# One TensorE run per chunk: x rows, state products, scores, log sums and transposes on small tiles, from the 11th chunk on

## The chip, the cores and the metric

The kernel runs on one core of one Trainium2 chip. The metric is the device time of one execution in microseconds (us). The time before the change is 608.76 us, the median of three runs between 608.49 and 609.51.

## What is computed

The first part is a gated linear recurrence over 768 steps for 4 batches of 8 heads of width 48; the second part is a layer with 2048 hidden units over all 3072 rows.

```python
f = 1.0 / (1.0 + np.exp(-f_logit))
for t in range(S):                       # q, k, v, f_logit: (4, 8, 768, 48)
    state = f[:, :, t, :, None] * state + np.einsum('bhd,bhe->bhde', k[:, :, t], v[:, :, t])
    y[:, :, t] = np.einsum('bhd,bhde->bhe', q[:, :, t], state)
x = y.transpose(0, 2, 1, 3).reshape(B * S, H * D)     # (3072, 384)
h = x @ w_in                                          # w_in (384, 2048)
sp = np.maximum(h, 0.0) + np.log1p(np.exp(-np.abs(h)))
out = (h * erf(sp)) @ w_out                           # w_out (2048, 384)
```

All of it is fp32.

## The kernel before

The rows are cut into 24 chunks of 128 steps (six per batch), and two chunks make a block of 256 rows, so there are 12 blocks. For each chunk the recurrence is worked out in matrix form, in two halves of 64 steps. These are the stages of one chunk `g`, with the lines under which the profile shows them:

- **Log sums** (`log_sums`, L396): one 128x128 by 128x384 matmul with the triangular matrix `tri` sums the logarithms of the gates `lt` over each half. `decays` (L400, L401) are two exponentials of it on ScalarE, and VectorE multiplies them into q (`times_q`, L414) and k (`times_k`, L421). `send_totals` (L408) sends the totals of the halves out with eight small DMAs on SP's queue.
- **Transposes** (`transposes`, L437): eight 128x128 transposes turn the decayed q and k into columns. ScalarE copies q (`copy_q`, L443), VectorE copies k (`copy_k`, L451).
- **State products** (`state_products`, L499): k times v, sixteen 64x48 matmuls on tiles of 64 rows and 64 columns of TensorE; the results lie in the PSUM tile `sc`, one bank for each half. **Scores** (`scores`, L510): sixteen 48x64 matmuls into the same tile. VectorE masks the scores (L537) and adds up the state (`add_state`, L475 and L476), and GpSimd copies the state into `sv` (`copy_state`, L481). The state of the second half is put off in `late` and runs ahead of a later stage.
- **Rows of x** (`x_rows`, L580): 32 matmuls of 128 rows by 32 columns give the chunk's output, called `y`; `copy_x` (L591) copies it on ScalarE into `xT`.

The second part works on blocks. `hidden` (L671) gives the 2048 hidden units of a block in four groups of 12 matmuls; ScalarE copies each group out of PSUM (L683), and `act_steps` takes it through the activation on ScalarE and VectorE in small steps. `project` (L822) makes the output of a block with 56 products of 128x192. Hidden groups and outputs use one pool of two PSUM buffers of two banks, `ps_moe`; log sums, transposes and y use another, `ps_at`, of two buffers of one bank.

The order is written out by hand (`manual_schedule`), so every engine gets its instructions in the order of the source. The first chunks follow a list of tokens (`EARLY`). After it, an iteration `it` runs the output products of block `it - 2` and the hidden groups of block `it + 1`, and after each matmul, a slot `s`, the loop may put in something else: a step of an activation, a sum for the output stage, a load, or a stage of the chunks of block `it + 2`. From block `ADJACENT = 5` (chunk 10) on, the stages stand at these slots of the 104 of an iteration, where `stage_y_s` is the x rows of a chunk, followed directly by state products and scores of the next one:

```python
todo += [(stage_y, g)] if last else [(stage_d, g + 1), (stage_t, g + 1), (stage_y_s, g)]
at = [0, 1, 15, 24, 31, 52, 66] if it + 2 == ADJACENT else [2, 26, 42, 54, 76, 90]
```

The last chunk's y stands at slot 54 of the ninth iteration, among the last output products. Loads of q, k, v and of the gate logits (`load`, `load_f`) and of v into `sv` (`load_sv`, L256) go through SP's queue in the order in which they are issued.

Of the kernel before, what the change touches and what calls it, by code (L numbers as in the profile page):

```python
# [70 lines left out]
P = 128  # L71
# [3 lines left out]
def kernel(  # L75
# [44 lines left out]
    for i, a in enumerate(a for _, a, _ in SERF_KAB):  # L120
        nc.vector.memset(serf_bias[:, i : i + 1], a)

    def heads(src, b, c):
        return src[b, :, c * P : (c + 1) * P, :].rearrange("h t d -> t h d")

# [49 lines left out]
    epool = main.enter_context(tc.tile_pool(name="epool", bufs=2))  # L175
    work1 = main.enter_context(tc.tile_pool(name="work1", bufs=1))
    ps_sc = main.enter_context(tc.tile_pool(name="ps_sc", bufs=1, space=PSUM))
    ps_at = main.enter_context(tc.tile_pool(name="ps_at", bufs=2, space=PSUM))
    ps_moe = main.enter_context(tc.tile_pool(name="ps_moe", bufs=2, space=PSUM))

    sc_all = ps_sc.tile([P, 2, 512], FP32, name="sc", tag="sc")

# [35 lines left out]

    FIRST, TOTALS = 3, 6


    lts = {}

    def load_f(g):
        b, c = divmod(g, NCH)
        blk, j = divmod(g, CPB)
        if blk not in lts:
            lts[blk] = lpool.tile([P, CPB, d_model], FP32, name="lt", tag="lt")
        nc.sync.dma_start(
            out=lts[blk][:, j, :].rearrange("t (h d) -> t h d", d=D), in_=heads(f_logit, b, c)  # L230
        )

    def load(g, what="qkv", queue=None):
        b, c = divmod(g, NCH)
# [4 lines left out]
        if "v" in what:  # L239
            queue.dma_start(  # L240
                out=vts[g % NV][:].rearrange("t (h d) -> t h d", d=D), in_=heads(v, b, c)
            )

    def half(c):
        return slice(C * c, C * (c + 1))

    def copy_sv(g, r, c):
        pairs = vts[g % NV][half(c)].rearrange("t (a r d) -> t a r d", r=2, d=D)
# [141 lines left out]
    def log_sums(g):  # L390
        blk, j = divmod(g, CPB)
        if g < FIRST:
            dTs[g] = pair_tile()[:, 0, 0:d_model]
        else:
            dTs[g] = ps_at.tile([P, 512], FP32, name="ps_d", tag="at")[:, 0:d_model]
        nc.tensor.matmul(dTs[g], lhsT=tri[:], rhs=lts[blk][:, j, :], start=True, stop=True)  # L396

    def decays(g):
        ps = dTs.pop(g).rearrange("t (h d) -> t h d", d=D)
        nc.scalar.activation(out=dps[g % 2][:, :, 0:D], in_=ps, func=AF.Exp, scale=-1.0)  # L400
        nc.scalar.activation(out=kds[g % 2][:, :, 0:D], in_=ps, func=AF.Exp)  # L401

    def send_totals(g):
        dp = dps[g % 2]
# [17 lines left out]
            out=kd, in0=kns[g % NQ][:].rearrange("t (h d) -> t h d", d=D), in1=kd, op=ALU.mult  # L422
        )

    def stage_d(g):
        log_sums(g)
        decays(g)
        send_totals(g)
        times_q(g)
        times_k(g)  # L430

    def transposes(g, n):
        src = qd if n == "q" else kds[g % 2]
        tps[g, n] = ps_at.tile([P, HP, P], FP32, name="ps_t", tag="at")
        flat = src[:].rearrange("t (a r) d -> t a (r d)", r=2)
        for a in range(HP):
            nc.tensor.transpose(tps[g, n][:, a, :], flat[:, a, :], ident[:])  # L437

    def copy_q(g):
        qAs[g] = work.tile([P, 2, HP, P], FP32, name="qA", tag="qA")  # L440
        ps = tps.pop((g, "q"))
        for r in range(2):
            nc.scalar.copy(out=qAs[g][half(r), r], in_=ps[half(r)])  # L443

    def copy_k(g):
        kTs[g] = work1.tile([P, HP, P], FP32, name="kT", tag="kT")
        ps = tps.pop((g, "k"))
        if g < 9:
            nc.scalar.copy(out=kTs[g][:], in_=ps[:])
        else:  # L450
            nc.vector.tensor_copy(out=kTs[g][:], in_=ps[:])  # L451

    def stage_t(g):
        if g - 1 in late:
            late.pop(g - 1)()
        transposes(g, "q")
        transposes(g, "k")
        copy_q(g)
        copy_k(g)

# [28 lines left out]
    def no_state(g):  # L489
        for r in range(2):  # L490
            nc.gpsimd.memset(svs[g % NSV][rows(r), r, 0, :, PAD : PAD + D], 0.0)
# [57 lines left out]
    def stage_s(g):  # L549
        n = g % NCH  # L550
        if n == 0:
            no_state(g)
        state_products(g)
        scores(g)
        for c in range(2):
            for r in range(2):
                mask(g, c, r)
                if c == 1 and by_select(g):
                    select(g, r)
        next_state(2 * g)  # L560
        if n < NCH - 1:
            late[g] = lambda: next_state(2 * g + 1)

    def x_rows(g, c):
        if c == 0:
            yts[g] = (
                pair_tile()[:, 0, 0 : n_k * P].rearrange("t (k n) -> t k n", k=n_k) if g < 2
                else ps_at.tile([P, n_k, P], FP32, name="y", tag="at")
            )
        y, qA, sv = yts[g], qAs[g], svs[g % NSV]  # L570
        todo = {i: [] for i in range(P // M)}
        for kt in range(n_k):
            for i in todo:
                a, part = divmod(kt * (P // M) + i, 3)
                for r, o in {0: ((0, PAD),), 1: ((0, PAD + M), (1, 0)), 2: ((1, M),)}[part]:
                    todo[i].append((kt, a, r, o))
        for n in range(len(todo[0])):
            for i in todo:
                kt, a, r, o = todo[i][n]
                nc.tensor.matmul(  # L580
                    y[M * i : M * (i + 1), kt, half(c)], lhsT=sv[:, r, c, a, o : o + M],
                    rhs=qA[:, r, a, half(c)], start=(c == 0 and n == 0), stop=True,
                    skip_group_check=True,
                )
# [8 lines left out]
    def stage_y(g):  # L593

        if g in late:
            late.pop(g)()
        x_rows(g, 0)
        x_rows(g, 1)
        copy_x(g)

    def stage_y_s(g):

        stage_y(g)
        stage_s(g + 1)


    acts = deque()
# [180 lines left out]
    def project(blk):  # L788
# [7 lines left out]
        }.items()}  # L796
        first = [1, 2, 5, 3]
        if end:
            place[4] = ps_at.tile([P, 512], FP32, name="ops4", tag="at")[:, 0:DH]
            first.append(4)  # L800

        def pair(n):
# [79 lines left out]
    def check_decays():  # L882

        low = work.tile([P, 1], FP32, name="low", tag="low")
        nc.vector.tensor_reduce(
            out=low[:], in_=Tall[:].rearrange("p g c a -> p (g c a)"), axis=AX.X, op=ALU.min
        )
        yield
        ps = ps_at.tile([P, 512], FP32, name="ps_f", tag="at")
        nc.tensor.transpose(ps[0:1, 0:P], low[:], ident[:])  # L890
        low1 = work.tile([1, 1], FP32, name="low1", tag="low1")
        nc.vector.tensor_reduce(out=low1[:], in_=ps[0:1, 0:P], axis=AX.X, op=ALU.min)
        nc.vector.tensor_scalar(
            out=flag[0:1, :], in0=low1[:], scalar1=GUARD, scalar2=None, op0=ALU.is_lt
        )
        yield
# [84 lines left out]
    with tc.manual_schedule():  # L981
# [39 lines left out]
            if to_load and home_free(to_load[0]):  # L1021
                load_piece(to_load.pop(0))

        def load_to(g):
            while loaded[0] <= min(g, n_chunks - 1):
                load(loaded[0])
                loaded[0] += 1


        LOOK = 3  # L1030
        loaded = [2 * ADJACENT + 1]

        nc.vector.memset(sc_all[:, :, HP * C : HP * (C + D)], 0.0)
        busy.append(ps_moe.tile([P, 2, 512], FP32, name="busy", tag="moe")[:, 0, 0:P])
        early()

        def stages(blk):
            todo = [(stage_s, blk * CPB)] if blk == ADJACENT else []
            for g in range(blk * CPB, (blk + 1) * CPB):
                last = g == n_chunks - 1  # L1040
                if blk >= ADJACENT:
                    todo += [(stage_y, g)] if last else [(stage_d, g + 1), (stage_t, g + 1), (stage_y_s, g)]
                    continue
                todo += [] if last else [(stage_d, g + 1)]
                todo += [(stage_s, g)]
                todo += [] if last else [(stage_t, g + 1)]
                todo += [(stage_y, g)]
            return todo

        check = check_decays()  # L1050
        due = 0.0
        for it in range(2, n_blocks):
            gen, n = slots(it)
            todo = stages(it + 2) if it + 2 < n_blocks else []
            at = [int(3 + (n - 13) / max(1, len(todo)) * i) for i in range(len(todo))]
            if ADJACENT <= it + 2 < n_blocks:

                at = [0, 1, 15, 24, 31, 52, 66] if it + 2 == ADJACENT else [2, 26, 42, 54, 76, 90]
                at = at[: len(todo)]
            if it + 3 < n_blocks:  # L1060
                prepare_at = at[todo.index((stage_d, (it + 3) * CPB))] - 14
            at, todo = deque(at), deque(todo)
            for s, _ in enumerate(gen):
                due += 0.6
# [5 lines left out]
                if at and s == at[0]:  # L1070
                    at.popleft()
                    f, g = todo.popleft()
                    f(g)
                    if f in (stage_y, stage_y_s):
                        if g + NSV < n_chunks:
                            load_sv(g + NSV)
                        load_to(g + LOOK)
                if s == n // 2 and it + 4 < n_blocks:
                    for j in range(CPB):
                        load_f((it + 4) * CPB + j)  # L1080
                if it + 3 < n_blocks and s == prepare_at - 6:
                    clamp(it + 3, 0, CPB)
                if it + 3 < n_blocks and s == prepare_at:
                    logs(it + 3, 0, CPB)
                if it < 4:
                    step = s % 7 in (1, 4)
                elif it == n_blocks - 1:
# [236 lines left out]
```

## Time and profile before

The execution under the profiler took 610.34 us; its span on the core is 608.6 us, so some 1.7 us lie around it.

| engine | busy us | share of the span |
|---|---|---|
| TensorE (PE) | 590.3 | 97% |
| weight loads (PEld, beside PE) | 517.1 | 85% |
| VectorE (DVE) | 430.2 | 71% |
| ScalarE (ACT) | 382.8 | 63% |
| GpSimd (POOL) | 92.3 | 15% |

| group of TensorE | records | busy us |
|---|---|---|
| hidden units (L671) | 1152 | 259.7 |
| x rows y (L580) | 1408 | 25.4 |
| log sums (L396) | 48 | 19.6 |
| scores (L510) | 768 | 16.3 |
| state products (L499) | 704 | 14.0 |
| transposes of k, of q (L437) | 96, 96 | 15.1, 14.6 |

A record is one instruction on the engine: an fp32 matmul makes two, a transpose one. Busy times of records overlap where several tiles of the array work at once, so a group's busy time is not what it takes away from the rest; for that, the starts in the timeline are compared. Idle time of an engine counts only where TensorE waits for it.

### The profile page before, as it was taken

How to read it: one execution, taken by the hardware profiler on the slowest of the kernel's cores; microseconds unless marked ns; L12 is line 12 of the kernel's file. 1: busy time of each engine (PE TensorE's matmuls, PEld its weight loads, DVE VectorE, ACT ScalarE, POOL GpSimd, SP SyncE). 2: the span in 40 equal slices, each digit the busy share in tenths (PEclk: the TensorE clock that was granted, in tenths of full speed). 3: DMA queues.
4: the chain of work that ended last, by engine and by line, in shares of the span. 5: the costliest groups of instructions: out<-in, count | busy, mean ns of one | idle time of the engine just before them, and what ended most of it. 6: DMA issues, size and time to landing. Idle time of an engine off the chain costs nothing.

```text
span 608.6 us, 13919 instructions
## 1 busy us (share of the span) xinstructions
PE 590.3 (97%) x5769; PEld 517.1 (85%) x5769; DVE 430.2 (71%) x705; ACT 382.8 (63%) x483; POOL 92.3 (15%) x119
## 2 busy tenths in 40 slices
PE   8999999998899999999999999999999899999995
PEld 7788888886566789889989889989989789989995
DVE  4789889976975876867776677767686575648451
ACT  6738859787836687757757766857676446366000
POOL 1330342120404010220021200112011200000000
PEclk9999999999899999999999999999999999999998
DMA  9799966206130430520421421412310000000000
GB/s 187 211 234 238 236 146 128 32 2 156 32 74 2 99 59 1 105 53 3 89 57 14 79 57 24 80 41 40 54 41 1 2 26 1 27 1 2 27 26 30
DMA packets 152148, 41.34 MB, mean 68 GB/s; under 512 B 143888, under 2 KB 146960, under 8 KB 152080
## 3 DMA queue, kind: packets, MB, share of 16 engines
q1 hardware_dynamic: 149856, 39.81, 29.9%
q8 instruction: 47, 0.77, 0.5%
q10 hardware_dynamic: 2224, 0.59, 0.4%
q14 instruction: 21, 0.17, 0.1%
HBM read 35.59 MB, written 4.72 MB: 66 GB/s over the span
## 4 chain that ended last, share of the span: by engine, by line
PE 82%; DVE 6%; ACT 6%; DMA 2%; issue 1%; POOL 1%; SPq 1%; ACTq 0%; DVEq 0%; POOLq 0%
PE hps L671 36%; PE ops L822 25%; PE ops L771 6%; PE y L580 3%; PE ps_t L437 3%; PE ps_d L396 2%; PE sc L510 2%; PE sc L499 2%; PE busy L380 1%; ACT x L160 1%; DMA w_out_sb<-in_moe_w_out_dram 1%; DVE e L165 1%; POOL sv L481 1%; DVE qA L537 1%; DVE Hg L628 1%
## 5 line engine op out<-in xcount | busy, mean ns | idle before, releaser
L671 PE MATMUL hps<-xT,w_in_sb 128*128 128x256 f32 x1152 | 259.7, 383 | 2.4 <-ACT Hg L683 1.7
L671 PEld LDWEIGHTS hps<-xT,w_in_sb 128*128 128x128 f32 x1152 | 217.6, 191 | 34.5 <-ACT Hg L683 2.1
L165 DVE SCALAR_TENSOR_TENSOR e<-x,e 128x1024 f32<-128x1024 f32 x96 | 117.4, 1223 | 15.7 <-ACT x L160 15.3
L481 POOL COPY sv<-state 48x192 f32<-48x192 f32 x88 | 75.8, 861 | 340.7 <-DVE state L476 245.6
L160 ACT ACTIVATE x<-Hg,serf_bias 128x1024 f32<-128x1024 f32 x88 | 97.5, 1141 | 0.2
L157 ACT ACTIVATE e<-Hg 128x1024 f32<-128x1024 f32 x44 | 46.5, 1058 | 57.3 <-DVE Hg L628 57.1
L822 PE MATMUL ops<-wT,Hg 128*128 128x192 f32 x320 | 78.5, 329 | 0.0
L683 ACT COPY Hg<-hps 128x1024 f32<-128x1024 f32 x44 | 44.4, 1010 | 42.7 <-PE hps L671 42.5
L628 DVE TENSOR_TENSOR Hg<-Hg,e 128x1024 f32<-128x1024 f32 x44 | 53.7, 1221 | 24.5 <-ACT e L625 24.4
L822 PE MATMUL ops<-wT,scratch 128*128 128x192 f32 x288 | 67.9, 327 | 0.9 <-DVE scratch L830 0.9
L822 PE MATMUL ops<-w_out_sb,Hg 128*128 128x192 f32 x320 | 65.1, 326 | 0.0
L822 PEld LDWEIGHTS ops<-wT,Hg 128*128 128x128 f32 x320 | 55.8, 190 | 1.9
L822 PEld LDWEIGHTS ops<-w_out_sb,Hg 128*128 128x128 f32 x320 | 54.6, 190 | 2.0
L537 DVE TENSOR_TENSOR qA<-sc,tri 64x256 f32<-64x256 f32 x68 | 28.7, 422 | 35.7 <-PE sc L510 31.6
L625 ACT ACTIVATE e<-e 128x1024 f32<-128x1024 f32 x48 | 50.4, 1051 | 2.9 <-DVE e L165 2.8
L822 PEld LDWEIGHTS ops<-wT,scratch 128*128 128x128 f32 x288 | 50.3, 190 | 1.1 <-issue 1.1
L830 DVE TENSOR_TENSOR scratch<-scratch,ops 128x384 f32<-128x384 f32 (+1 forms) x40 | 19.9, 497 | 34.1 <-ACT scratch L838 26.6
L443 ACT COPY qA<-ps_t 64x512 f32<-64x512 f32 x48 | 27.8, 578 | 13.1 <-PE ps_t L437 12.7
L414 DVE TENSOR_TENSOR qd<-qn,dp 128x384 f32<-128x384 f32 x24 | 13.9, 579 | 28.6 <-ACT dp L400 28.6
L822 PE MATMUL ops<-w_out_sb,scratch 128*128 128x192 f32 x132 | 32.3, 326 | 0.0
L580 PEld LDWEIGHTS y<-qA,sv 128*32 128x32 f32 x1408 | 21.2, 110 | 8.7 <-issue 5.4
L838 ACT COPY scratch<-ops 128x192 f32<-128x192 f32 x10 | 3.2, 318 | 39.2 <-PE ops L822 39.2
(123 smaller groups left out, 692.6 us busy)
## 6 DMA issues: line engine op xcount, KB each, us to landing
lt<-in_f_logit_dram SPq DMA_DIRECT2D x24, 192.0 KB, 3.8
qn<-in_q_dram SPq DMA_DIRECT2D x24, 192.0 KB, 3.9
kn<-in_k_dram SPq DMA_DIRECT2D x23, 192.0 KB, 3.5
vt<-in_v_dram SPq DMA_DIRECT2D x23, 192.0 KB, 4.0
out_dram<-scratch SPq DMA_DIRECT2D x11, 384.0 KB, 2.6
sv<-in_v_dram SPq DMA_DIRECT2D x84, 48.0 KB, 2.9
w_out_sb<-in_moe_w_in_dram SPq DMA_DIRECT2D x4, 768.0 KB, 7.3
Hg<-in_moe_w_in_dram SPq DMA_DIRECT2D x4, 768.0 KB, 6.4
```

Of the source, the lines that this page charges most:

```text
L157: nc.scalar.activation(out=dst[:], in_=h, func=AF.Exp)
L160: nc.scalar.activation(out=dst[:], in_=h, func=AF.Tanh, bias=serf_bias[:, i : i + 1], scale=SERF_KAB[i][0])
L165: nc.vector.scalar_tensor_tensor(out=e[:], in0=x[:], scalar=SERF_KAB[i][2], in1=e[:], op0=ALU.add, op1=ALU.mult)
L481: nc.gpsimd.tensor_copy(out=svs[g1 % NSV][rows(r), r, c1, :, PAD : PAD + D], in_=state[rows(r)])
L537: nc.vector.tensor_tensor(out=to, in0=sc[half(c), r], in1=tri1[half(c)].unsqueeze(1).broadcast_to((C, HP, C)), op=ALU.mult,)
L580: nc.tensor.matmul(y[M * i : M * (i + 1), kt, half(c)], lhsT=sv[:, r, c, a, o : o + M], rhs=qA[:, r, a, half(c)], start=(c == 0 and n == 0 ...
L625: nc.scalar.activation(out=e[0][:], in_=e[0][:], func=AF.Tanh, scale=SERF_C)
L628: nc.vector.tensor_tensor(out=h, in0=h, in1=e[0][:], op=ALU.mult)
L671: nc.tensor.matmul(hts[blk, gi][:, j, :], lhsT=w_in_sb[:, kt, ft * P : (ft + 1) * P], rhs=xTs[blk][:, kt, :], start=(kt == 0), stop=(kt == ...
L683: nc.scalar.copy(out=gr["h"], in_=hts.pop((blk, gi))[:])
L771: nc.tensor.matmul(ops[:, tt, 0:d_model], lhsT=gr["h"][:, j, tt * P : (tt + 1) * P], rhs=w_out_sb[:, ft, :], start=(ft == 0), stop=(ft == ...
L822: nc.tensor.matmul(place[n], lhsT=x[:, j, :], rhs=y, start=(gi == 0 and j == 0 and n in first), stop=(gi == n_g - 1 and j == 1), skip_grou ...
```

## The change

From chunk 10 on, one function `burst(g)` replaces the three places of a chunk. It issues on TensorE, one after the other, the x rows of chunk `g`, the state products and scores of `g + 1`, the log sums of `g + 3` and the transposes of `g + 2`. It stands at two slots of an iteration: after the first hidden group of 12 matmuls and after the last slot.

- The log sums of chunks 13 to 23 are four matmuls of 64x64 tiles with 192 columns each, into a buffer of `ps_moe`. For this the gate logits lie otherwise in `lt`: four heads in each half of the partitions, the two halves of the chunk beside each other, loaded with four DMAs in place of one. Chunks 11 and 12 keep the former log sums.
- The transposes of chunks 11 to 23 are sixteen of 64 rows, into two banks, one for each half. Those of chunk 11 stand alone at slot 15 of the third iteration, as before.
- The two one-bank buffers `ps_at` are closed before chunk 11 and one buffer of two banks, `ps_at2`, takes their place; y lies in its first bank, the transposes in both.
- The loads of q and k run one chunk further ahead, those of the gate logits about an iteration, and the state of the second half is updated eight slots after the run.

Everything up to the state products of chunk 10 keeps its order. The core of the diff:

```diff
+    singles = ExitStack()
+    ps_at = [singles.enter_context(tc.tile_pool(name="ps_at", bufs=2, space=PSUM))]
+    def bank(name):
+        if len(ps_at) == 1:
+            return ps_at[0].tile([P, 512], FP32, name=name, tag="at")
+        return bank_pair(name)[:, 0, :]
+    def bank_pair(name):
+        return ps_at[1].tile([P, 2, 512], FP32, name=name, tag="at2")
+    def open_pair():
+        singles.close()
+        ps_at.append(main.enter_context(tc.tile_pool(name="ps_at2", bufs=1, space=PSUM)))
...
+    MERGE = 2 * ADJACENT
+    SPLIT = MERGE + 3
...
+        if g < SPLIT:
+            nc.sync.dma_start(out=lt.rearrange("t (h d) -> t h d", d=D), in_=heads(f_logit, b, c))
+            return
+        w = d_model // 2
+        for n in range(2):
+            for u in range(2):
+                t0 = c * P + u * C
+                nc.sync.dma_start(
+                    out=lt[half(n), w * u : w * (u + 1)].rearrange("t (h d) -> t h d", d=D),
+                    in_=f_logit[b, HP * n : HP * (n + 1), t0 : t0 + C, :].rearrange("h t d -> t h d"),
+                )
...
+    def tiled_sums(g):
+        blk, j = divmod(g, CPB)
+        w = d_model // 2
+        dTs[g] = ps_moe.tile([P, 2, 512], FP32, name="ps_d", tag="moe")[:, :, 0:w]
+        for i in range(2):
+            for c in range(2):
+                n = (c + i) % 2
+                nc.tensor.matmul(
+                    dTs[g][half(c), n, :], lhsT=tri1[half(n), :],
+                    rhs=lts[blk][half(n), j, w * c : w * (c + 1)], start=True, stop=True,
+                )
...
+    def tiled_transposes(g):
+        ps = bank_pair("ps_t")
+        for i, src in enumerate((qd, kds[g % 2])):
+            part = ps[:, :, HP * C * i : HP * C * (i + 1)]
+            for a in range(HP):
+                for c in range(2):
+                    nc.tensor.transpose(
+                        part[:, c, C * a : C * (a + 1)], pairs(src)[half(c), a, :],
+                        ident[half(c), half(c)],
+                    )
+            tps[g, "qk"[i]] = part.rearrange("p c (a t) -> p a c t", a=HP)
...
-    def stage_y_s(g):
-        stage_y(g)
-        stage_s(g + 1)
+    def burst(g):
+        if g in late:
+            late.pop(g)()
+        x_rows(g, 0)
+        x_rows(g, 1)
+        s, t, d = (n < n_chunks for n in (g + 1, g + 2, g + 3))
+        if s:
+            if (g + 1) % NCH == 0:
+                no_state(g + 1)
+            state_products(g + 1)
+            scores(g + 1)
+        if d:
+            tiled_sums(g + 3)
+        copy_x(g)
+        if t:
+            tiled_transposes(g + 2)
+        if s:
+            masks(g + 1)
+        if d:
+            decays(g + 3)
+            send_totals(g + 3)
+        if t:
+            copy_q(g + 2)
+            copy_k(g + 2)
+        if d:
+            times_q(g + 3)
+            times_k(g + 3)
...
+            first = [(stage_s, g), (stage_d, g + 1), (stage_t, g + 1), (stage_d, g + 2)]
+            return (first if blk == ADJACENT else []) + [(burst, g), (burst, g + 1)]
...
+            loads, logits_at = {n - 20: it + 5}, {36: it + 4}
+            if it == 3:
+                loads[6], logits_at = it + 4, {8: it + 3, 34: it + 4}
...
-                at = [0, 1, 15, 24, 31, 52, 66] if it + 2 == ADJACENT else [2, 26, 42, 54, 76, 90]
+            if it >= 3:
+                if it == 3:
+                    open_pair()
+                at = ([0, 1, 15, 24] if it == 3 else []) + [n - 1 - 3 * n_h // 4, n - 1]
...
+                        load_to(g + LOOK)
+                        load_to(g + LOOK + (f is burst), 1)
+                        late_at = 8
...
+                if it >= 3 and late and not late_at:
+                    late.pop(min(late))()
+                late_at -= 1
```

## The prediction

> **What bounds the kernel now.** I read the busy shares first, then the slices, then the waits of TensorE, then TensorE's timeline around one chunk. The page says who is full:
>
> ```profile
> PE 590.3 (97%) x5769; PEld 517.1 (85%) x5769; DVE 430.2 (71%) x705; ACT 382.8 (63%) x483; POOL 92.3 (15%) x119
> ...
> PE   8999999998899999999999999999999899999995
> ```
>
> TensorE is busy in nearly every slice, and the chain that ended last is 82% PE. From 210 us on, which is all of the stretch that the change touches, its own waits are two:
>
> ```profile
> PE y L580 <- POOL sv L481: 1.6, 1, 1.6
> PE ops L822 <- DVE scratch L830: 0.9, 1, 0.9
> ```
>
> So time moves only by TensorE work that gets shorter or longer, by the first of these waits, or by a new wait. The timeline shows what one chunk costs TensorE (start, length, engine, line, tiles, shape, records; an fp32 matmul is two records, a transpose one):
>
> ```profile
> 305.02 0.60 PE L437 MATMUL ps_t<-ident,qd 128*128 128x128 f32 x4
> 305.46 0.60 PE L437 MATMUL ps_t<-ident,kd 128*128 128x128 f32 x4
> 305.90 6.21 PE L671 MATMUL hps<-xT,w_in_sb 128*128 128x256 f32 x28
> 312.04 1.10 PE L580 MATMUL y<-qA,sv 128*32 128x64 f32 x64
> 313.07 0.57 PE L499 MATMUL sc<-vt,kd 64*48 64x48 f32 x32
> 313.46 0.66 PE L510 MATMUL sc<-qA,kT 48*64 48x64 f32 x32
> 314.05 5.88 PE L671 MATMUL hps<-xT,w_in_sb 128*128 128x256 f32 x26
> ...
> 320.74 0.81 PE L396 MATMUL ps_d<-lt,tri 128*128 128x384 f32 x2
> 321.39 0.81 PE L822 MATMUL ops<-w_out_sb,Hg 128*128 128x192 f32 x4
> ```
>
> Differences of starts are the true cost, since lengths overlap. The eight transposes: 305.90 - 305.02 = **0.88 us**. The log sums: 321.39 - 320.74 = **0.65**. The run of y, state products and scores: 314.05 - 312.04 = 2.01, plus its edges. A hidden record takes 0.216 us (25 records in 299.63 to 305.02 on the same timeline), so 28 end at 311.94 and y starts 0.10 late; the 26 records after it take 5.72 in place of 5.61, another 0.11. Together **2.2**. One chunk: 2.2 + 0.88 + 0.65 = 3.73 us.
>
> How parallel are small tiles here? A hidden record streams 256 columns in 0.216 us, 0.84 ns a column, so 64 columns are 54 ns. The 64 y records take 1.03 us less a change of tile shape of about 0.1: 14.5 ns each, 3.7 at a time. The state products: 0.39 / 32 = 12.2 ns against 48 columns at 40 ns, 3.3 at a time. Four 64x64 tiles do run side by side.
>
> **What the Trainium skill says.** "TensorEngine Tiling (Array Packing)", Key Properties: changing the tiling mode drains TensorE, and different tiles may load weights and multiply in parallel. The trace agrees with both: about 0.1 us before y, 0.1 from y to the state products, 0.1 after the return, none between state products (64*48) and scores (48*64), and the 3.3 to 3.7 at a time above. The same page, Gotcha 1 of Restrictions and Gotchas: row tiles must write different PSUM banks. State products do so now (the two halves of `sc`), and the new forms do too (banks n and c). "TensorE: Matmul & The Clock Gate", LDWEIGHTS: a weight load takes about columns / 1.2 ns, whatever the rows. The groups agree (110, 121, 135, 190 ns for 32, 48, 64, 128 columns: 0.83 ns a column over a fixed 83), but the transposes' own loads are 142 ns for 128 columns: 59 over the fixed part, so these stream twice as fast. The same page, Part 1: a gate halves the clock after a window of little work, about 3.4 us. Here once late:
>
> ```profile
> 482.00:486.00 4.00, 2.75 (x38) 2.23 (x39) 2.03 (x4) 2.61 (x4) 1.44 (x2) 0.82 0.01 4
> 486.00:490.00 4.00, 4.00 (x16) 3.32 (x15) 3.93 (x7) 1.75 (x2) 0.00 (x0) 0.75 0.28 100
> ```
>
> The column after POOL is the granted clock. It falls right after y of chunk 23 waited 1.61 us at 483.15 for the state copy on POOL, and costs 4 x 0.18 + 4 x 0.25 = 1.7 us.
>
> **The change part by part.** (a) Log sums of chunks 13 to 23 (11): one 128x384 matmul becomes four of 64x64 with 192 columns. Two records of 192 x 0.84 = 162 ns per tile, four tiles at once: 0.33 us, a gain of 0.32 each. If only two run at once it is 0.65, no gain. No row shows four 64x64 tiles with 192 columns; the state products and scores are nearest, and I take their parallelism.
>
> (b) Transposes of chunks 11 to 23 (13): eight of 128 rows become sixteen of 64 rows and 64 moving columns, on two row tiles. Streaming alone is 8 x 54 ns = 0.43; loads of 59 ns per tile with some 6 ns between (scores: (0.59 - 0.11) / 8 = 60 ns a group of four for 54) give 8 x 65 = 0.52. If loads of the two row tiles don't overlap it is 16 x 59 = 0.94, slightly worse than now. I take 0.52: gain 0.36 each.
>
> (c) Edges. The run keeps those of today and adds one, from 64x64 to 64-row tiles with 128 columns, ahead of the transposes: unseen, between 0 (the state products and scores switch freely) and 0.2 (the dearest edge's two parts); I take the 0.13 of the known ones. Chunk 11's transposes stand alone between 128x128 work and pay both outer edges, 0.3.
>
> (d) Sum: 11 full runs (chunks 10 to 20) x (0.32 + 0.36 - 0.13) = 6.05; the run of chunk 21 has no log sums: 0.36 - 0.13 = 0.23; chunk 11's transposes 0.36 - 0.3 = 0.06. Together **6.3 us** off TensorE, all on the path. The bounds are 13 x 0.45 + 11 x 0.32 - 0.3 = 9.1, with the new edge free, and -13 x 0.06 - 12 x 0.2 - 0.3 = -3.5.
>
> (e) Placement. Runs now stand after the first hidden group and after the last one. Chunk 23's y comes 36 hidden matmuls (36 x 0.43 = 15.6 us) after chunk 22's, not 12 products (3.9 us). The state copies let y go on at 483.15, 8.4 us after chunk 22's y began at 474.79, so the wait goes: **1.6 us**. With it probably the half clock: 1.7 in this execution. But the execution shown took 610.34 (span 608.6 and 1.7 around it), 1.6 above the median of 608.76, and the unprofiled runs may lack that window, so I count half: **0.85**.
>
> (f) New waits in a run. Transposes need both banks that y held, so they wait for ScalarE's copy of y. Ahead of that copy stands the copy of the hidden group (1.01 us), which starts about 0.2 after the group's last record streams, and y's own copy (0.48) may then start at 1.2 us into the run and ends at 1.75. TensorE gets to the transposes at 0.1 + 1.03 + 0.39 + 0.48 + 0.33 + edges = 2.4. Cover 0.65 us; ScalarE was idle before most group copies (42.5 us over 26). Gone, it costs the excess, up to one activation of 1.15 us. The log sums take a hidden/output PSUM buffer: its last readers are VectorE's final sums of the output stage, over 7 us earlier. The next hidden group needs the buffer of the first, free after 1.2 us, inside the run. The reverse wait, for the two decay activations, has 5.2 us of hidden matmuls over it.
>
> (g) Other engines. Copies, decays, masks and sums keep their sizes. VectorE gets them in a lump (masks 4 x 0.42, state 0.75, key copy 0.69, products 1.13: 4.3 us) that puts off hidden activations behind it; these are needed one block later (46 us). The log loads of 11 chunks become four issues each, 33 more on SP's queue at about 0.75 us (`sv` loads, 2.73 for 4): 6 us per block in place of 1.7, ahead of the next totals and value loads; SP then has 2 x 10.3 (totals 5.2, `sv` 2.7, q, k and v 2.4) + 6 = 27 of a block's 46 us, and all of it is needed half a block later. Cost nothing. The second half of each state update moves 8 slots behind the run, off its head: nothing, as TensorE doesn't wait there now.
>
> Total: against the profiled execution's own 610.34, 6.3 + 1.6 + 1.7 = 9.6 off, 600.7. Against the median, with half of the clock, 8.75 off: 608.76 becomes **600.0**.
>
> **The rivals.** R1: the row tiles' weight loads don't overlap, so the transposes gain nothing: 13 x 0.36 = 4.7 less, **604.7**. For it: no transposes on row tiles in this trace, and they have a special load. Against: state products load and multiply on four tiles in 49 ns. R2: the log sums don't overlap either and the run only moves: another 11 x 0.32 = 3.5, **608.2**. R3: y's copy comes late in most runs, 0.6 us in each of 12: **607.2**. R4, slower: a run of 3.2 us of small tiles and edges lowers the clock as at 484.55. Each half window costs 1.7 us; from the sixth of the 12 runs on (6 x 1.7 = 10.2 against 8.75) it decides, and in all of them gives 600.0 + 20 = **620**. Against: from 24 to 36 us TensorE ran mostly such small tiles, at a clock of 1.00.
>
> **How the numbers follow.** The forecast has 0.62, with its own range of 596.8 to 602.5 (the free edge and the whole clock below, an edge of 0.2 and no clock above). R1 0.17, R3 0.08, R2 0.04, R4 0.07, and 0.02 for a transfer or other wait that I don't see, put on the slow side. A measurement tells about 0.2%, 1.2 us, from no change: R2 falls inside, R4 and the unseen are slower, R3 is just outside on the fast side. So faster 0.87, same 0.04, slower 0.09. The range reaches over R1 and the milder half of R3: 596.8 to 606.0.
>
> **What would show each step.** The groups: 44 log-sum matmuls as 88 records of 64*64, 64x192, and 208 transposes of 64 rows. On the timeline of a run: log sums to transposes 0.33 us, transposes to the next 128x128 record 0.5 and an edge; 0.85 or more there is R1. Waits of TensorE for the y copy are R3. The clock of 461 to 508 should read 1.00, and no y wait for POOL; clocks below 0.95 in the middle windows are R4. I am wrong if the middle blocks (46.4 us now, 275.16 to 321.55 from first product to first product on the chain) shrink by less than 0.6 us.

## The result and the profile after

The changed kernel took **603.37 us**, the median of four runs (603.09 to 604.60), against 608.62 of the kernel before in four runs beside it (608.34 to 609.51): a ratio of 0.9922, 95% interval 0.9894 to 0.9950. The forecast was 600.0. Two later comparisons gave smaller gains: 604.54 against 607.28 (0.9966, 0.9950 to 0.9982) and 604.57 against 607.62 (0.9944, 0.9924 to 0.9965). The recorded ratios differ a little from the quotients of these medians. Executions of one kernel differ in how many windows of half clock they hold (the last section comes back to this), so only medians of one comparison, or kernels with like medians of before beside them, are set against each other below.

The execution profiled after the change took 603.14 us. Its page says that TensorE works less and is as full as before:

```profile
span 601.4 us, 14264 instructions
PE 581.5 (97%) x5939; PEld 507.6 (84%) x5939; DVE 429.6 (71%) x705; ACT 382.9 (64%) x483; POOL 103.5 (17%) x119
```

One run of the middle of the program, on TensorE's timeline (start, length, engine, line, tiles, shape, records):

```profile
300.01 1.10 PE L650 MATMUL y<-qA,sv 128*32 128x64 f32 x64
301.05 0.57 PE L565 MATMUL sc<-vt,kd 64*48 64x48 f32 x32
301.44 0.66 PE L576 MATMUL sc<-qA,kT 48*64 48x64 f32 x32
301.92 0.51 PE L435 MATMUL ps_d<-lt,tri 64*64 64x192 f32 x8
302.36 0.46 PE L494 MATMUL ps_t<-ident,qd 64*128 64x64 f32 x8
302.66 0.42 PE L494 MATMUL ps_t<-ident,kd 64*128 64x64 f32 x8
303.00 15.81 PE L765 MATMUL hps<-xT,w_in_sb 128*128 128x256 f32 x72
```

Starts again: the log sums 302.36 - 301.92 = 0.44 us, their 0.33 and part of an edge; the sixteen transposes 303.00 - 302.36 = 0.64, of which 0.50 stream (by the 62 ns between pairs within a group) and the rest is the return to 128x128. Blocks without a wait take 45.27 us from first product to first product (323.13 to 368.40), two chunks each, where they took 46.39: 0.56 us per run, and the forecast had 0.55.

The waits of TensorE from 190 us on, where there were two (what waits, for what: us in total, times, longest):

```profile
PE ps_t L494 <- ACT xT L661: 1.9, 2, 1.1
PE hps L765 <- ACT Hg L777: 1.2, 1, 1.2
PE ps_t L494 <- issue: 1.1, 1, 1.1
PE ops L916 <- DVE scratch L924: 0.9, 1, 0.9
PE hps L765 <- DVE scratch L924: 0.8, 2, 0.6
```

The wait of y for GpSimd is gone, the fourth line is the old one, and the four others are new. They have taken back most of what TensorE saved. On the timeline, taking each gap beyond the usual pitch and the usual 0.25 us edge ahead of the transposes (so a little more than the waits, as the pipeline also refills): 1.17 us in the run of chunk 10 at 208.57, 1.33 before a hidden matmul at 221.00, 0.92 in the run of chunk 11 at 229.64, 0.76 and 0.34 before hidden matmuls at 249.34 and 387.05, and 1.1 inside the transposes at 322.93. Together **5.6 us**.

ScalarE's timeline shows why the run of chunk 10 waits:

```profile
201.86 1.28 ACT L380 ACT_TABLE_LOAD   x1
203.16 0.84 ACT L400 ACTIVATE lt<-lt 128x768 f32<-128x768 f32 x1
204.03 0.84 ACT L401 ACTIVATE lt<-lt 128x768 f32<-128x768 f32 x1
204.88 1.28 ACT L719 ACT_TABLE_LOAD   x1
206.18 1.06 ACT L719 ACTIVATE e<-e 128x1024 f32<-128x1024 f32 x1
207.14 0.99 ACT L777 COPY Hg<-hps 128x1024 f32<-128x1024 f32 x1
208.03 0.48 ACT L661 COPY xT<-y 128x384 f32<-128x384 f32 x1
```

The rows of y began at 205.07 and were ready about 206.1. Their copy starts at 208.03, because two loads of function tables, exp and ln of the logits (L400, L401), one activation (L719) and the copy of the hidden group (L777) stand ahead of it. The transposes need both banks of y, so TensorE waits until the copy is through.

### The profile page after: what moved, and what is told of

Read it like the earlier page. It is cut to its first block, busy times and chain, and to the rows that moved or that the text cites. A ratio compares the mean times of both kernels' runs of the same rounds, so it can differ in the third digit from the quotient of the medians.

```text
span 601.4 us, 14264 instructions
## 1 busy us (share of the span) xinstructions
PE 581.5 (97%) x5939; PEld 507.6 (84%) x5939; DVE 429.6 (71%) x705; ACT 382.9 (64%) x483; POOL 103.5 (17%) x119
## 4 chain that ended last, share of the span: by engine, by line
PE 73%; ACT 12%; DVE 6%; DMA 3%; issue 2%; SPq 2%; POOL 1%; ACTq 0%; DVEq 0%
PE hps L765 33%; PE ops L916 22%; PE ops L865 5%; PE y L650 3%; ACT x L163 3%; PE sc L576 2%; PE sc L565 2%; PE ps_t L494 1%; DMA vt<-in_v_dram 1%; PE ps_t L484 1%; DVE Hg L722 1%; SPq L451 1%; ACT e L160 1%; DVE e L168 1%; ACT Hg L777 1%
## 5 line engine op out<-in xcount | busy, mean ns | idle before, releaser
L547 POOL COPY sv<-state 48x192 f32<-48x192 f32 x88 | 87.2, 991 | 337.1 <-DVE state L542 285.2
L777 ACT COPY Hg<-hps 128x1024 f32<-128x1024 f32 x44 | 44.4, 1009 | 44.6 <-PE hps L765 44.2
L719 ACT ACTIVATE e<-e 128x1024 f32<-128x1024 f32 x48 | 50.3, 1048 | 2.8 <-DVE e L168 2.8
L650 PE MATMUL y<-qA,sv 128*32 128x64 f32 x1408 | 25.0, 221 | 1.0 <-POOL sv L547 0.9
```

Source lines behind the costliest of these rows:

```text
L547: nc.gpsimd.tensor_copy(out=svs[g1 % NSV][rows(r), r, c1, :, PAD : PAD + D], in_=state[rows(r)])
L650: nc.tensor.matmul(y[M * i : M * (i + 1), kt, half(c)], lhsT=sv[:, r, c, a, o : o + M], rhs=qA[:, r, a, half(c)], start=(c == 0 and n == 0 ...
L719: nc.scalar.activation(out=e[0][:], in_=e[0][:], func=AF.Tanh, scale=SERF_C)
L777: nc.scalar.copy(out=gr["h"], in_=hts.pop((blk, gi))[:])
```

## The experiments

Twelve runs follow, two of them the changed kernel again. They fall into three groups of four that each share runs of the kernel before, with medians of 607.28, 607.45 and 607.62.

### Parts of the change undone

**The move alone**: runs at their new places, but with one plain 128x384 log sum ahead of the run, eight plain transposes at its end, and the gate logits loaded as before (`SPLIT`).

```diff
-    SPLIT = MERGE + 3
+    SPLIT = n_chunks
...
+        ps = ps_moe.tile([P, 2, 512], FP32, name="ps_d", tag="moe")[:, 0, 0:d_model]
+        nc.tensor.matmul(ps, lhsT=tri[:], rhs=lts[blk][:, j, :], start=True, stop=True)
...
+                nc.tensor.transpose(part[:, a, :], pairs(src)[:, a, :], ident[:])
...
+        if d:
+            tiled_sums(g + 3)
         x_rows(g, 0)
         x_rows(g, 1)
...
-        if d:
-            tiled_sums(g + 3)
         copy_x(g)
```

> The run of a chunk stands where the change puts it, but both small-tile forms are undone: one 128x384 log-sum matmul at the head of the run, eight 128x128 transposes at its end. Theory (the small tiles bring some 0.55 us a run, and new waits for ScalarE take part of it back): each clean run is about 3.74 us, as the three places before cost together, so 11 x 0.54 + 0.3 = 6.2 us over the changed kernel, less up to 1.5 because the transposes start later and wait less for y's copy: 608 to 609.6 us, no faster than before. Rival (the gain comes from gathering the work in one place, fewer changes of tile shape, and the wait of chunk 23 that goes): at most 605 us.

Measured: 609.34, ratio to before 1.0035 (1.0020 to 1.0051): slower than before, and 4.8 us slower than the changed kernel beside it. So the small tiles are worth about 5 us, near the 6.3 of step (d), and the move by itself, which also frees y of chunk 23, loses. Its trace has waits at the same places as the changed kernel, at 208.56, 220.99, 229.63, 249.72 and 389.14. Its blocks without a wait take 46.3 us (277.91 to 324.21), as before the change (46.39), so what it loses lies in these waits and in a stop at 397.87.

**Log sums plain**, **transposes plain**: one half of that edit each, the first with the log sum at the head of the run.

> Only the tiled log sums are undone: one 128x384 matmul at the head of the run, where TensorE still works on 128x128 tiles, with the gate logits loaded as before the change. Theory (four 64x64 tiles run side by side): 0.65 in place of 0.33 us in 11 runs, +3.5, less some 0.6 of waits for y's copy that the longer head covers: about 606.3 us. Rival (tiles of one matmul wait for each other): no change, 603.4.

Measured: 607.21 (1.0001, 0.9982 to 1.0021), 2.7 us slower than the changed kernel, where 2.9 was expected: 11 x 0.32 = 3.5 by step (a), less 0.6 of waits that the longer head covers.

> Only the 64-row transposes are undone: eight of 128x128, at the same place in the run, into the same two banks (q in one, k in the other). Theory: 0.88 us in place of 0.50 and an edge of 0.165 from 64x64 to 64x128 tiles, +0.21 in 12 runs and some 0.1 for chunk 11: +2.6, about 606.0 us. Rival (the edge eats the whole gain of the transposes): no change, 603.4; if the edge were free: +4.6.

Measured: 604.49 (0.9959, 0.9943 to 0.9974), no different from the changed kernel. That is a miss. On its timeline the run does get longer: from the first transposes to the next hidden matmul 305.07 - 304.14 = 0.93 us in place of 0.64, and a block takes 45.65 in place of 45.27, 0.19 per run, some 2.2 us in all. But the stop of 1.1 us inside the transposes at 322.93 is not there. So 1.1 of the 2.2 is accounted for; the rest lies within what these comparisons can tell.

> The changed kernel itself once more, beside the three others: 603.4 us. By the theory of a late ScalarE its profile shows TensorE's waits for y's copy in the runs of chunks 10 and 11 (1.1 and 0.85 us) and for the copy of a hidden group at 221 us (1.2) again, since they follow from the order of ScalarE's instructions; the stop of 1.1 us inside the transposes at 322.9 us, for which the profile names nothing, should come again at the same place if it hangs on the program and not on the execution.

Measured: 604.54 (0.9966). Every wait named above came again within 0.6 us of its place: 208.27, 220.70, 229.35, 249.05, 322.51, 386.63. Their places belong to the program, not to the execution. The size of the stop near 322.5 does not: 1.13 us idle in the first trace, 0.86 in this one.

### y of chunk 23 alone

```diff
                 at = at[: len(todo)]
+                if it + 3 == n_blocks:
+                    at[3] = n - 1
```

> The kernel before with one line changed: y of chunk 23 is issued at the last slot of its block, 36 hidden matmuls later. Nothing of the computation changes. Theory (step (e) of the prediction): y's wait of 1.6 us for the state copy goes, and with it the half clock behind it: 1.6 us faster than before, up to 3.3 where the half clock was there too. Rival (the wait was a feature of the one execution profiled, or x of chunk 23, now late, is waited for in its place): within 0.5 us of before.

Measured: **604.27** against 607.45 (0.9956, 0.9940 to 0.9972), 3.2 us between the medians from one line changed in the kernel before, as much as the whole change gave in the groups of runs ahead of and behind this one (2.7 and 3.1). Its only wait of TensorE from 190 us on is the old one:

```profile
PE ops L822 <- DVE scratch L830: 0.9, 1, 0.9
```

The clock of 478 to 490 us reads 1.00. The wait itself was 1.6. A half clock behind it in some executions of the kernel before would account for more, and the mean clocks of the runs fit that: they are at or below 0.994 in 18 of the 37 runs of before and in 2 of these 17. With half of the 1.7 the gain would be 2.45; the ratio of 0.9956 is 2.7 us, its interval 1.7 to 3.6. Only one execution of before was traced, so where its low clocks lie is inferred.

### ScalarE's work elsewhere

```diff
-            loads, logits_at = {n - 20: it + 5}, {36: it + 4}
+            loads, logits_at = {n - 20: it + 5}, {44: it + 4}
             if it == 3:
-                loads[6], logits_at = it + 4, {8: it + 3, 34: it + 4}
+                loads[6], logits_at = it + 4, {8: it + 3, 27: it + 4}
```

> The changed kernel with ScalarE's exp and ln of the logits put elsewhere: in all later blocks at slot 44 in place of 36, in the block of chunks 10 and 11 at slot 27 in place of 34. Nothing of the computation changes. Theory (the change's own new waits on ScalarE: two table loads, exp and ln, some 3.5 us, stand ahead of a copy that TensorE waits for): the waits of the runs of chunks 10 and 11 (1.4 and 1.2 us) lose about 1 us together and the two waits of the hidden matmuls for the output buffer (0.76 and 0.34) go; 1 to 2 us faster than the changed kernel. Rival (ScalarE is just behind, whatever stands where): the waits only change place and the time stays within 0.5 us.

Measured: 601.13 (0.9898, 0.9874 to 0.9922), about 3.4 us less than the changed kernel has in its two groups; more than expected. The waits at 208, 249 and 387 are gone, the one at 221 falls from 1.33 to 0.73, the one at 229 stays at 0.92. So the order of ScalarE's instructions was the cause of those that went; the wait at 229 was not touched by this.

### The stop that waits for nothing

In four traces (the changed kernel twice, the move alone, log sums plain) TensorE idles for 0.67 to 1.13 us in the midst of small tiles, with "issue" as its releaser: the profile shows no semaphore that holds it. Counting all records of TensorE ahead of the stop (matmuls, weight loads, and the semaphore instructions of its sequencer) gives 7105, 7105, 8385 and 5569. All leave 193 when divided by 256. And each stop ends 2.3 to 2.6 us after a transfer of 16,384 bytes starts on queue q8, the page's "instruction" queue (320.31 and 322.92 in the changed kernel). The Trainium skill, "Runtime: NRT & Kernel Launch", section Instruction fetch mechanics, says that instructions are refilled in 16 KiB blocks of 256, fetched while the current one runs, with the cost of crossing "mostly hidden". Hidden work takes 0.216 us for two records, 28 us a block. A run issues 256 of them in 1.9 us.

If that is the cause, a stop comes only where one block's edge lies early in a run and the next near its end, and shifting the program by a few instructions moves it. The run of chunk 10 has idle time to shift in: the log sums of chunk 13 are issued several times there, with the same values.

```diff
-        for i in range(2):
+        for i in range(2 * 2 if g == SPLIT else 2):    # 2 * 5 in the other kernel
```

> The changed kernel with the four log-sum matmuls of chunk 13 issued twice (same values into the same place), inside the run of chunk 10, where TensorE waits 1.4 us for ScalarE anyway. All later TensorE instructions come 16 records later. Theory (a run of small tiles outruns the loading of instructions, which comes in blocks of 256: a stop is where a block's edge falls early in a run and the next edge near its end): the stop at 322.5 shrinks and others appear in the transposes of the runs near 276, 367 and 413 (and perhaps 458), 0.4 to 1.1 us each; 2.5 to 4.0 of stops in all in place of 1.1, so 1.4 to 3 us slower than the changed kernel. Rival (the stop belongs to the place in the program, or to chance): one stop near 322.5 as before, same time within 0.4.

> As the run before it, but the four log-sum matmuls of chunk 13 are issued five times: 64 records later, 1.3 us of work in the 1.4 us of the wait. Theory (blocks of 256 instructions): no run has an early edge, so no stop of 0.3 us or more is left between 230 and 470; 0.8 to 1.2 us faster than the changed kernel, although TensorE has 16 matmuls more to do. Rival: stop as before; the added work costs 0 to 0.3 us.

The timelines around the edges: first two pieces of the kernel with the sums twice, then one of the kernel with five:

```profile
275.56 0.35 PE L494 MATMUL ps_t<-ident,kd 64*128 64x64 f32 x5
277.10 0.33 PE L494 MATMUL ps_t<-ident,kd 64*128 64x64 f32 x3 [1.19 <-issue]
...
367.91 0.43 PE L916 MATMUL ops<-w_out_sb,Hg 128*128 128x192 f32 x1
369.49 0.76 PE L916 MATMUL ops<-w_out_sb,Hg 128*128 128x192 f32 x3 [1.15 <-issue]
```

```profile
321.53 0.46 PE L494 MATMUL ps_t<-ident,qd 64*128 64x64 f32 x8
321.83 0.41 PE L494 MATMUL ps_t<-ident,kd 64*128 64x64 f32 x8
322.18 0.92 PE L916 MATMUL ops<-w_out_sb,Hg 128*128 128x192 f32 x4
```

Sixteen records more: the stop near 322 is gone and two others stand at 277.10 and 369.49, two of the places forecast; 413 and 458, forecast too, show none. Ahead of these two stops are 6081 and 8129 records: again 193 when divided by 256, only at other edges. (So it is for the stops of three more traces at 7105: the logits elsewhere, the changed kernel a third time, and the first of the two kernels at the end of this section; and for five smaller ones, 0.16 to 0.47 us, in four traces, at 6081, 9153 and 10177.) Sixty-four records more: no stop anywhere. Times: 603.98 and **602.12**. The kernel with more matmuls is 1.9 us faster than its neighbour and some 2.4 below the changed kernel of the other groups, against an expected 0.8 to 1.2. The kernel with the sums twice was expected 1.4 to 3 us slower than the changed kernel and, across groups, is 0.6 faster: its direction is a miss, though its trace has the stops; it also lost 0.3 us of the wait at 208 and the wait at 387. Where the stops are follows the count of instructions. Whether there is one, and how long, depends on more: in the kernel with the sums five times a block of 256 records is through at 366.33 in 1.85 us without a stop, and no 16,384 byte transfer starts inside it. That TensorE stops where it reaches a block whose transfer began too shortly before is the reading that fits; the fetch itself was not changed.

### The edge between tile shapes

```diff
-        if d:
-            tiled_sums(g + 3)
         copy_x(g)
         if t:
             tiled_transposes(g + 2)
+        if d:
+            tiled_sums(g + 3)
```

> The changed kernel again, beside the three that follow on the same chip: the value that they are compared with. One stop of 1.1 us near 322.5 and the waits of the runs of chunks 10 and 11 as before; 603 to 605 us.

> The changed kernel with the log sums behind the transposes of the run in place of ahead of them: TensorE then goes from 64x64 tiles to 64x128, back to 64x64, and to 128x128, one change of tile shape more in each of the 11 full runs. Nothing of the computation changes. Theory (step (c): a change of tile shape costs 0.13 to 0.17 us): 11 x 0.15, 1.7 us slower than the changed kernel, or less where the wait for y's copy, now 0.3 us earlier in the run, eats or adds something. Rival (the edge was only the first row's slower weight load, which any order has): same within 0.5.

Measured: 604.57 for the changed kernel, 606.53 for this one, **2.0 us** more. The changed kernel did not have the one stop of 1.1 us that was expected: it has 0.58 us at 323.07 and two more, 0.47 and 0.45, at 415.51 and 461.51. The run of the other kernel:

```profile
304.46 0.66 PE L576 MATMUL sc<-qA,kT 48*64 48x64 f32 x32
305.05 0.47 PE L494 MATMUL ps_t<-ident,qd 64*128 64x64 f32 x8
305.35 0.42 PE L494 MATMUL ps_t<-ident,kd 64*128 64x64 f32 x8
305.70 0.56 PE L435 MATMUL ps_d<-lt,tri 64*64 64x192 f32 x8
306.18 1.99 PE L765 MATMUL hps<-xT,w_in_sb 128*128 128x256 f32 x8
```

From the scores to the hidden matmuls it takes 306.18 - 304.46 = 1.72 us, in the changed kernel 303.00 - 301.44 = 1.56. The edge more costs 0.16, eleven times 1.8. Its waits from 190 us on add up to 7.0 us, against 6.3 in the trace of the changed kernel beside it, so of the 2.0 us not all need be the edge; the 0.16 on the timeline doesn't depend on them.

### A version without the waits

The logits elsewhere as above, and chunk 11's copy of y on VectorE, which idles there; then, in the second kernel, chunk 11's transposes plain as well, for 16 records less and so another position of the blocks.

```diff
-        nc.scalar.copy(out=xTs[blk][:, :, j * P : (j + 1) * P], in_=yts.pop(g)[:])
+        copy_by(nc.vector if g == MERGE + 1 else nc.scalar, xTs[blk][:, :, j * P : (j + 1) * P], yts.pop(g)[:])
...
+            if g == MERGE + 1:          # second kernel only
+                part = ps[:, i, :].rearrange("p (a t) -> p a t", a=HP)
+                for a in range(HP):
+                    nc.tensor.transpose(part[:, a, :], pairs(src)[:, a, :], ident[:])
+                tps[g, "qk"[i]] = part.rearrange("p a (c t) -> p a c t", c=2)
+                continue
```

> The changed kernel with the logits' exp and ln at the other slots (as in the earlier run) and chunk 11's copy of y on VectorE in place of ScalarE. Theory (step (f)'s mis-sizing is ScalarE's lateness in a few places): of the waits of 1.4, 1.3, 1.2, 0.8 and 0.3 us some 0.7 us is left, near 219; about 4 us faster than the changed kernel, with the stop of 1.1 near 320 still there. Rival: VectorE's copy comes behind its own work and the wait moves to the masks or activations behind it; no faster than with the logits moved alone.

> As the run before it, and chunk 11's transposes plain (8 of 128 rows in place of 16 of 64): 8 fewer matmuls and 8 fewer weight loads, all later TensorE instructions 16 records earlier, which by the positions of the 256-instruction blocks leaves no early edge in any run. Theory: the stop near 320 goes, 1.1 us faster than the run before it; 598 to 600 us. Rival: the stop stays, same within 0.3.

Measured: 600.15 (0.9876, 0.9857 to 0.9896) and **598.28** (0.9850, 0.9832 to 0.9868), 4.4 and 6.3 us below the changed kernel beside them. The first still has its stop, 1.4 us with "issue" at 324.46. In the second, all waits of TensorE from 190 us on are:

```profile
PE ops L922 <- DVE scratch L930: 0.9, 1, 0.9
PE hps L771 <- ACT Hg L783: 0.6, 1, 0.6
```

It is 9.3 us faster than the kernel before beside it. So with the waits and the stop out of the way nothing is left of the shortfall: steps (a) to (e) of the prediction had 8.75.

## Why the prediction came out as it did

The sign and the range (596.8 to 606.0) held. The point, 600.0, was 3.4 us low, and the likeliest case's own range ended at 602.5, 0.9 short. That the range held by 2.6 us is in part luck: taken off 608.76, the gains of the two later comparisons end at 606.0 and 605.7, at its very edge. (The ends of the likeliest case's range lie 0.8 us outside what its stated terms give, 597.6 and 601.7.)

**Steps (a) to (d) were right in size.** Log sums, transposes and the added edge were forecast at 0.33, 0.52 and 0.13 us a run and came out at 0.33, 0.50 and 0.16; the gain per run was forecast at 0.55 and came out at 0.56. Four 64x64 tiles and two row tiles do overlap, so R1 and R2 are out: the transposes' 16 records take 0.50 us and not the 0.94 of R1. The trace keeps agreeing with "TensorEngine Tiling (Array Packing)" in the Trainium skill, Key Properties, by which a change of the tiling mode drains TensorE: the one edge that was added costs 0.16 us, and switching between the 64*48 and 48*64 tiles costs nothing visible.

**Step (e) was right.** The wait went. The half clock was counted half, 0.85, and the line tried alone, with an interval of 1.7 to 3.6 us, fits the 2.45 that this makes. The ground given for the half was weaker than it looked: that the profiled execution was 1.6 us longer than the median need not be that window, as it also has 6.68 us after its last matmul where the other fourteen traces have 4.90 to 4.99.

**Step (f) failed**: it looked at the new waits in a run and put them at nothing. The cover of 0.65 us was worked out for a ScalarE that is idle when the group's copy comes due. In most runs it was right: none from chunk 12 on waits for y's copy. But its own figure, ScalarE idle before 26 group copies, leaves 22 of the 48 before which ScalarE had work. It was not asked what stands on ScalarE's queue at the two first runs, where the same iteration has the logits of two blocks and an activation every 3.5 slots. They cost 1.17 and 0.92, each near the "up to one activation of 1.15" that the step itself named as its bound. R3 had this mechanism with 0.6 us in each of 12 runs; it is 1.0 in two.

**Step (g) failed in part.** It had VectorE get its work in a lump and put that at nothing. After the run of chunk 10 ScalarE waits 3.21 us for VectorE and then copies the next hidden group too late:

```profile
217.81 1.06 ACT L160 ACTIVATE e<-Hg 128x1024 f32<-128x1024 f32 x1 [3.21 <-DVE Hg L722]
219.94 1.01 ACT L777 COPY Hg<-hps 128x1024 f32<-128x1024 f32 x1
```

TensorE goes on at 221.00, 1.33 us late. Moving the logits took away 0.6 of it; the lump itself was not tried apart, so that it causes the rest is not shown. The moved stages also changed the order on ScalarE around the logits: before, the small copy of the output stage (L838, at 241.71) came just ahead of the table load; after, it comes at 248.38 behind it, and the buffer that the next hidden matmul needs stays full, 0.76 us. With the logits at other slots this wait was gone.

**What no step had**: the stop of 1.1 us with "issue" as its releaser. The trace of before has none from 190 us on.

The sum: 6.3 of (d) and 2.45 of (e) less 5.6 of waits and stop leave 3.1 us. Measured were 5.25, 2.7 and 3.1. A half-clock window that costs 1.7 of 605 us takes 0.003 off the mean clock, so executions with 0.999 or more have none; among these it should be 6.3 + 1.6 - 5.6 = 2.3, and in the second comparison 12 of before have a median of 605.92 and 5 of the changed kernel one of 603.27, 2.65 apart, near that. Why the first comparison has 2 us more stays open: its four runs of before took 608.34 to 609.51, the later medians of before are 607.28 to 607.62, and the clocks of the four are not on record.

**R4 is out.** The granted clock of the stretch with the late runs (columns: PE, PEld, DVE, ACT, POOL busy, then the clock):

```profile
461.00:508.00 47.00, 47.00 (x415) 43.71 (x414) 32.57 (x50) 28.16 (x30) 7.73 (x6) 1.00 0.04 11
```

While TensorE works, the one half-clock window of this execution lies near 22 us, far from the runs. In the profiled execution of before, two lie at 156 and 484.

## What to carry to other kernels

Where small matmuls are joined into one run, the saving on TensorE can be read from the timeline to a tenth of a microsecond; what decides is the queue of the engine that must empty the PSUM banks in between, so walk that queue at each run, above all in the iterations that differ, and not on average. Try the cheapest part of a change alone: here one moved y was worth as much as all of it in two of three comparisons. And where a run of many tiny instructions stops for no semaphore, count the instructions ahead of it: some more or fewer moved or removed a stop of a microsecond here.

## What the runs showed of the hardware

- Where 256 records of small matmuls are used up in some 2 us, TensorE can stop with no semaphore to wait for: fourteen stops of 0.16 to 1.40 us in nine traces from 190 us on, all at the same remainder, 193, of the instruction count by 256, with a 16,384 byte transfer on the instruction queue starting 2.2 to 2.8 us ahead of the end of each. The "mostly hidden" quoted above fits the 28 us that a block of hidden matmuls lasts, and not these.
- Half-clock windows of 3.4 us, 1.7 us of time each, come in some executions and not in others of the same kernel: near 22, 156 or 484 us, and once for 6.8 us at 77. TensorE had been less busy just before those at 22, 156 and 484 (3.26, 1.93 and 2.30 of 4 us), but that alone does not bring one. The first line, of the kernel before, has a clock of 0.61 behind 1.93 busy us; in the changed kernel, in the two lines below, the clock stays at 1.00 behind 1.64:

```profile
156.00:160.00 4.00, 3.71 (x12) 2.66 (x13) 3.93 (x6) 3.92 (x8) 1.95 (x2) 0.61 0.52 98
```

```profile
152.00:156.00 4.00, 1.64 (x8) 0.78 (x8) 3.93 (x7) 3.94 (x7) 0.00 (x0) 1.00 0.16 13
156.00:160.00 4.00, 4.00 (x16) 2.54 (x16) 3.90 (x6) 3.32 (x5) 2.38 (x3) 1.00 0.47 86
```

- Of the first 63 later runs of the kernel before, those with a mean clock of 1.00 had a median of 605.75 us, those with 0.992 one of 607.93.
